# Modulation vectors on TensorE, or on VectorE from weights that the DMA has turned

## The chip, the core and the metric

The kernel runs on one core of a Trainium2 chip. Its time is the device time of one execution in microseconds (us); lower is better. TensorE multiplies matrices and writes PSUM, VectorE and ScalarE read PSUM back and do elementwise work, GpSimd (POOL in the profile) does small elementwise work and issues some DMAs, and SyncE (SP) issues most DMAs. Each engine runs its own queue in order.

## The reference

A transformer block of 2048 tokens and width 1024: linear attention with 32 heads, then a SwiGLU feed-forward of width 3584. Both halves are modulated by six vectors of 1024 that come from one conditioning vector `c`:

```python
mod = (silu(c) @ w_mod).reshape(1, 6, 1, 1024)
sa, ca, ga, sb, cb, gb = ...                       # the six vectors, in this order
h = layernorm(x) * (1 + ca) + sa
x = x + ga * A(h, wqkv, wo)                        # phi(q), phi(k), kv = sum k v, o = num/den, @ wo
h = layernorm(x) * (1 + cb) + sb
x = x + gb * B(h, w_gate, w_up, w_down)            # (silu(h@w_gate) * (h@w_up)) @ w_down
```

Here `w_mod` is 1024 x 6144. The change is about how `ga`, `sb` and `cb` are computed; `sa` and `ca` are needed at the very start and keep their way, and so does `gb`.

## The kernel before

The 2048 tokens are four blocks (`sc`) of 512. Activations stand transposed (`hT`: features on partitions, tokens along the row), so a modulation vector is wanted as columns (128 partitions x 8), one scalar to a partition, and `modulate` applies it with eight VectorE instructions to a block. The exception is the gate `ga`: it is folded into the weight `wo` (`wo * ga_bc`), for which it must stand as one row that all partitions hold (`ga_bc`).

**Phases of attention.** For each block: `k_phase` (eight groups of eight matmuls; each group's PSUM accumulator is taken by ScalarE's exp and two VectorE instructions, `phi_to`), `kv_phase` of the block before (128 small matmuls into one PSUM tile, added to `kv_acc` on VectorE), `v_phase` (eight groups, taken by ScalarE alone). While a block's k and v phases run, `ln1` prepares the next block: statistics on VectorE (`bn_stats`, `veps`), `rstd` and `nmr` on POOL, the normalised tile on ScalarE, a DMA transpose into `hT`, and `modulate`. After the last block come `q_phase(1, ...)`, the last `kv_phase`, the copies `KVB` and `Zden` on VectorE from `kv_acc`, a TensorE transpose `tpk` (tile `tp`) of `KVB`, the denominators `den`, and `fold_wo`, which multiplies `wo` by the kv matrix. Only then can attention's output `wo_tile` and the feed-forward (`gate_up`, `down`) run.

**The vectors before.** `mod_load` brings blocks of `w_mod` (tile `wml`) by plain DMAs. `ga_rows` and `mod_rows` multiply them on TensorE by silu(c) spread over 32 columns (`sc32`), 32 matmuls each into PSUM tile `modr`, with ScalarE copying the result out; POOL DMAs write rows to DRAM (`mrow_dram`) and read them back, broadcast for `ga_bc` and as columns for `sbT`, `cb1T`. They stand between two groups of `k_phase`: `ga_rows` in block 2, `mod_rows` in block 3.

**What sets the order.** A list scheduler orders each engine's instructions by priority, mostly program order. `mm` keeps TensorE in program order. `tc.issue_after(x)` puts an instruction behind `x`. `in_order` fixes the first block's order on VectorE, ScalarE and POOL. Two pools of PSUM accumulators, `pa` and `pb`, have four banks each: a matmul group cannot start until the group four before it has been taken out. The large SBUF tiles share 19 buffers (`k8`); a load waits until the tile that held its buffer has had its last use.

**The start.** `keep_warm` issues matmuls of zeros (`sel`) while the first DMAs are under way, so that TensorE's clock is up when the k matmuls of block 0 begin; `mod_rows_a` computes `sa` and `ca` as their weights (`wme`) land.

Of the kernel before, what the change touches and what calls it, by code (L numbers as in the profile page):

```python
# [9 lines left out]
ALU = mybir.AluOpType  # L10
BF16 = mybir.dt.bfloat16
# [10 lines left out]
def kernel(  # L22
# [91 lines left out]
    c_sb = const.tile([DC, P], BF16, name="c_sb")  # L114

    x_tiles = {}

    def load_x(st, eng):
        x_sb = k2.tile([P, D], BF16, name="x_sb")
        eng.dma_start(out=x_sb[:], in_=x2[st * P:(st + 1) * P, :])  # L120
        x_tiles[st] = x_sb

    for st in range(STC - 1):
# [61 lines left out]
    scr = scr_t[:, 0:A * 64].rearrange("p (i q r) -> p i q r", q=2, r=32)  # L185
    sa0T, ca0T = scr[:, :, 0, 0], scr[:, :, 1, 0]
    sbT = const.tile([P, DC], F32, name="sbT")
    cb1T = const.tile([P, DC], F32, name="cb1T")
    ga_t = ep.tile([P, NB], F32, name="e")
    ga_bc = ga_t[:].bitcast(BF16)  # L190
    gb_bc = const.tile([P, D], BF16, name="gb_bc")
# [9 lines left out]
    def build_masks():  # L201
        nc.gpsimd.memset(zmask[:], 0.0)
        for h in range(HPC):
            rs = slice(h * DH, (h + 1) * DH)
            for hg in range(HG):
                nc.gpsimd.memset(zmask[rs, hg, HG * h + hg:HG * h + hg + 1], 1.0)

    def rstd_of(mv, n):
        veps = small.tile([P, STC], F32, name="veps")
        nc.vector.tensor_scalar_add(out=veps[:, 0:n], in0=mv[:, 0:n, 1], scalar1=LN_EPS)  # L210
        rstd = small.tile([P, STC], F32, name="rstd")
        nc.gpsimd.tensor_tensor(out=rstd[:, 0:n], in0=veps[:, 0:n], in1=neg_half[:].to_broadcast([P, n]), op=ALU.pow)  # L212
        return rstd
# [9 lines left out]

    def normalise_act(dst, src, mv, rstd):
        nmr = small.tile([P, 1], F32, name="nmr")
        nc.gpsimd.tensor_scalar(out=nmr[:], in0=mv[:, 0, 0:1], scalar1=rstd[:, 0:1], scalar2=-1.0,  # L226
                                op0=ALU.mult, op1=ALU.mult)
        nc.scalar.activation(out=dst, in_=src, func=ACT.Identity, bias=nmr[:], scale=rstd[:, 0:1])  # L228

# [19 lines left out]
    def ln1_norm(sc, t, x_sb, mv, rstd, dve=False):  # L249
        xn = k2.tile([P, D], BF16, name="xn", bufs=4)  # L250
        if dve:
            normalise(xn[:], x_sb[:], mv[:, 0, 0:1], rstd[:, 0:1])
        else:
            normalise_act(xn[:], x_sb[:], mv, rstd)
        if sc > 0:
            nc.sync.dma_start_transpose(hTs[sc][:, :, t * P:(t + 1) * P], xn[:])
        return xn

    def ln1(sc):
# [48 lines left out]
    def k_phase(sc, lo, hi):  # L308
        if lo == 0:
            pks[sc] = big("pk", [STC, D])  # L310
        for g in k_groups[lo:hi]:
            accs = [acc_a()]
            k_mms(sc, [g], accs)
            k_evac(sc, [g], accs)

    def v_phase(sc):
        v = big("v", [VT + DH])
# [8 lines left out]
                                     start=(cc == 0), stop=(cc == DC - 1))  # L326
                nc.scalar.copy(out=v[:, t * D + nb * NB:t * D + (nb + 1) * NB], in_=acc[:])  # L327

    def q_phase(sc, lo=0, hi=DC):
        if lo == 0:  # L330
            pqs[sc] = big("pq", [HG, SCW])
        for qc in range(lo, hi):
            acc = acc_a()
            for cc in range(DC):
                mm(acc[:], lhsT=wq[cc // 4][:, cc % 4, qc * P:(qc + 1) * P], rhs=hTs[sc][:, cc, :],
                                 start=(cc == 0), stop=(cc == DC - 1))
            phi_to(pqs[sc][:, qc, :], acc[:])

    def v_ones(v, lo):
        head = v[:, lo:lo + DH]  # L340
# [2 lines left out]
    def kv_phase(sc):  # L343
        kvp = acc_b("kvp", (HG, 2, DH))
        for hg in range(HG):
            for t in range(STC):
                for i in range(HPC):
                    mm(kvp[i * DH:(i + 1) * DH, hg, :, :], lhsT=pks[sc][:, t, hg * P + i * DH:hg * P + (i + 1) * DH],
                       rhs=v_ones(vs[sc], t * D + hg * P + i * DH), start=(t == 0), stop=(t == STC - 1))
        kvv = kvp[:].rearrange("p g k e -> p g (k e)")[:, :, 0:DH + 1]  # L350
        if sc == 0:
            nc.vector.tensor_copy(out=kv_acc, in_=kvv)
        else:
            nc.vector.tensor_tensor(out=kv_acc, in0=kv_acc, in1=kvv, op=ALU.add)

    def gb_load():
        for j in range(DC):
# [9 lines left out]
            else:  # L367
                nc.vector.scalar_tensor_tensor(out=gb_acc[:], in0=t[:], scalar=sc, in1=gb_acc[:], op0=ALU.mult, op1=ALU.add)

    def ga_rows(blks):  # L370
        ps = acc_b("modr")
        H2 = NB // 2
        for j in range(DC):
            for g in range(4):
                mm(ps[32 * g:32 * g + 32, 0:H2], lhsT=sc32[:, j, :], rhs=blks[g // 2][:, j, (g % 2) * H2:(g % 2 + 1) * H2],
                   start=(j == 0), stop=(j == DC - 1))
        row = small.tile([P, NB], BF16, name="mrow", bufs=1)
        nc.scalar.copy(out=row[:, 0:H2], in_=ps[:, 0:H2])
        for g in range(4):
            nc.gpsimd.dma_start(out=mrow_dram[0, g:g + 1, 0:H2], in_=row[32 * g:32 * g + 1, 0:H2])  # L380
        nc.gpsimd.dma_start(out=ga_bc.rearrange("p (g n) -> p g n", g=4),
                            in_=mrow_dram[0, :, 0:H2].unsqueeze(0).to_broadcast([P, 4, H2]))

    gb_rows = []

    def mod_load(cols):
        blks = []
        for lo in cols:
            t = big("wml", [DC, NB])
            nc.sync.dma_start(out=t[:], in_=wm_v[:, :, lo:lo + NB])  # L390
            blks.append(t)
        return blks

    def mod_rows(blks):
        ps = acc_b("modr")
        for j in range(DC):
            for g in range(4):
                mm(ps[32 * g:32 * g + 32, :], lhsT=sc32[:, j, :], rhs=blks[g][:, j, :],
                                 start=(j == 0), stop=(j == DC - 1))
        row = small.tile([P, NB], BF16, name="mrow", bufs=1)  # L400
        nc.scalar.copy(out=row[:], in_=ps[:])
        return row

    mrow_dram = dram.tile([2, 4, NB], BF16, name="mrow_scratch")

    def mod_spread(k, row):
        for g in range(4):
            nc.gpsimd.dma_start(out=mrow_dram[k, g:g + 1, :], in_=row[32 * g:32 * g + 1, :])
        cols = small.tile([P, 2 * DC], BF16, name="mcol", bufs=1)
        with nc.allow_non_contiguous_dma(reason="2048 elements, once"):  # L410
            nc.gpsimd.dma_start(out=cols[:], in_=mrow_dram[1].rearrange("g (i p) -> p (g i)", p=P))
        nc.vector.tensor_copy(out=sbT[:], in_=cols[:, 0:DC])
        nc.vector.tensor_scalar_add(out=cb1T[:], in0=cols[:, DC:2 * DC], scalar1=1.0)

    def modulate_all(hT, scaleT, biasT):
        for cc in range(DC):
# [40 lines left out]
    def keep_warm(acc, n):  # L457
        for _ in range(n):
            mm(acc[:], lhsT=sel[:, 0, :], rhs=sel[:], start=True, stop=True)

    gs = k_groups[0:6]
    accs = [acc_a() if i < 4 else acc_b("acc") for i in range(6)]
    spare = accs[5]
    keep_warm(spare, 9)
    hT = hTs[0] = big("hT", [DC, SCW])
    pks[0] = big("pk", [STC, D])
    H = 3 * P
    with in_order(nc.vector, nc.scalar, nc.gpsimd):
# [6 lines left out]
        st0 = ln1_stats(0, 0)  # L475
        nc.vector.tensor_copy(out=sc32[:], in_=scT[:].unsqueeze(2).to_broadcast([P, DC, 32]))
        xns = [ln1_norm(*st0)] + [ln1_norm(*ln1_stats(0, t)) for t in range(1, 3)]
        keep_warm(spare, 6)
        mod_rows_a(0)
        pe_transpose_tile(hT, xns[0], 0)  # L480
        keep_warm(spare, 3)
        mod_rows_a(1)
        pe_transpose_tile(hT, xns[1], 1)
        keep_warm(spare, 2)
# [28 lines left out]
        k_evac(0, gs8, accs8)  # L513
    with tc.issue_after(last_on[nc.gpsimd.engine]):
        build_masks()
        nc.gpsimd.tensor_copy(out=scf[:], in_=scT[:])

    for sc in range(NSC):
        if sc > 0:
            k_phase(sc, 0, 2)  # L520
            kv_phase(sc - 1)
            k_phase(sc, 2, 4)
            if sc == 2:
                ga_rows(blks)
            if sc == 3:
                mod_spread(1, mod_rows(blks))
            k_phase(sc, 4, 8)
            if sc == 1:
                blks = mod_load([2 * D, 2 * D + NB])
            if sc == 2:  # L530
                blks = mod_load([3 * D, 3 * D + NB, 4 * D, 4 * D + NB])
        v_phase(sc)
        if sc + 1 < NSC:
            with tc.issue_after(last_on[nc.vector.engine] if sc == 0 else last_phi[-5].ins):
                ln1(sc + 1)
        if sc == 0:
            q_phase(0, 0, 6)
        if sc + 1 < NSC:
            with tc.issue_after(last_phi[0].ins):
                modulate_all(hTs[sc + 1], ca1T, saT)  # L540
        if sc == 0:
            q_phase(0, 6, 8)
        if sc + 2 < NSC:
            for st in range((sc + 2) * STC, (sc + 3) * STC):
                load_x(st, nc.sync)
        if sc == 2:
            wo = [big("wo", [4, D]) for _ in range(2)]
            for h in range(2):
                for g in range(4):
                    nc.sync.dma_start(out=wo[h][g * DH:(g + 1) * DH, :, :], in_=wo_v[h, g])  # L550
            for cc in range(DC):
                w = wo[cc // 4][:, cc % 4, :]
                nc.vector.tensor_tensor(out=w, in0=w, in1=ga_bc, op=ALU.mult)

    q_phase(1, 0, 2)
    kv_phase(NSC - 1)
    nc.vector.tensor_copy(out=KVB, in_=kv_acc[:, :, 0:DH])
    nc.vector.tensor_tensor(out=Zden[:], in0=kv_acc[:, :, DH:DH + 1].to_broadcast([P, HG, DH]),
# [121 lines left out]
    for st in range(STC):  # L680
        wo_tile(st)
    q_phase(2, 6, 8)
    q_phase(3, 0, 5)
    with tc.issue_after(last_phi[0].ins):
        modulate_all(h2Ts[0], cb1T, sbT)
# [63 lines left out]
```

## Time and profile before

| | us |
|---|---|
| median of 6 runs | 836.56 (836.3 to 837.0) |
| the profiled execution, its own time | 836.86 |
| its span, first to last instruction | 835.1 |
| TensorE busy | 823.9 |
| VectorE busy | 317.2 |
| ScalarE busy | 168.6 |
| GpSimd busy | 67.5 |
| bytes moved by DMA | 129.07 MB |

The page gives each engine's busy time, a chain of work that ended last (at each step, what released it), groups of equal instructions with the mean time of one and the idle time before them, and DMA issues with the time from issue to landing. A busy engine off the chain costs nothing; time on the chain that is taken away is gained only until the next wait shows. The granted TensorE clock was 1.0 over the span.

### The profile page before, as it was taken

The numbers are of one execution on the slowest core, as the hardware profiler recorded it, in microseconds if no ns is written. First come the engines' busy times: TensorE is split into PE (matmuls) and PEld (weight loads), VectorE is DVE, ScalarE is ACT, GpSimd is POOL, SyncE is SP. The second block draws the span as 40 slices with busy tenths as digits, with TensorE's granted clock in tenths as the row PEclk, the third lists the DMA queues.
The fourth block names the chain that finished last, engine by engine and source line by source line (L and its number), as shares of the span: only waits on it lengthen the run. The fifth ranks groups of instructions, "written<-read, shape, count | busy, mean of one in ns | idle before, by whom it ended". The sixth has DMA issues, their size and how long they took to land.

```text
span 835.1 us, 11191 instructions
## 1 busy us (share of the span) xinstructions
PE 823.9 (99%) x4560; PEld 378.3 (45%) x4641; DVE 317.2 (38%) x606; ACT 168.6 (20%) x253; POOL 67.5 (8%) x168
## 2 busy tenths in 40 slices
PE   8999999999999999999999999999999999999998
PEld 3444444444444444444444444444444444444444
DVE  5755643587444325521222244211114431111122
ACT  3455343334211111101111110111110101111000
POOL 2101201111130301100000010000001100000000
PEclk9999999999999999999999999999999999999999
DMA  9873790129998544636434183672504529710011
GB/s 319 298 202 85 226 197 1 31 62 287 358 261 257 189 151 139 189 112 221 147 108 144 44 227 95 216 224 79 174 1 154 162 69 329 241 54 1 19 58 51
DMA packets 125748, 129.07 MB, mean 155 GB/s; under 512 B 34112, under 2 KB 106304, under 8 KB 125184
## 3 DMA queue, kind: packets, MB, share of 16 engines
q1 hardware_dynamic: 121440, 114.97, 45.7%
q0 software_dynamic: 3968, 12.99, 5.3%
q8 instruction: 36, 0.59, 0.3%
q10 hardware_dynamic: 288, 0.40, 0.1%
q14 instruction: 16, 0.13, 0.0%
HBM read 108.27 MB, written 12.72 MB: 145 GB/s over the span
## 4 chain that ended last, share of the span: by engine, by line
PE 97%; DMA 2%; issue 1%; DVE 0%; ACT 0%; ACTq 0%; SPq 0%
PE acc L98 89%; PE a_ps L98 7%; DMA wme<-in_w_mod_dram 2%; PE kvp L98 1%; PE modr L98 0%; PE den L98 0%; PE mod_ps L98 0%; DVE wo L577 0%; PE wf L98 0%; DVE pq L292 0%; ACT eb L289 0%; ACTq L125 0%; PE tp L101 0%; SPq L134 0%; DVE eb L290 0%
## 5 line engine op out<-in xcount | busy, mean ns | idle before, releaser
L98 PE MATMUL acc<-h2T,wgu 128*128 128x512 bf16 x1756 | 385.7, 379 | 1.9
L98 PEld LDWEIGHTS <-wgu 128*128 128x128 bf16 x1792 | 175.1, 98 | 211.5
L98 PE MATMUL acc<-wd,gu 128*128 128x512 bf16 (+2 forms) x908 | 195.2, 373 | 0.9
L646 DVE TENSOR_TENSOR gu<-acc,e 128x512 bf16<-128x512 f32 x112 | 77.4, 691 | 289.9 <-PE acc L98 278.9
L645 ACT ACTIVATE e<-acc 128x512 f32<-128x512 f32 x112 | 66.9, 597 | 374.8 <-PE acc L98 363.4
L98 PEld LDWEIGHTS <-gu 128*128 128x128 bf16 x924 | 89.3, 98 | 104.5
L98 PEld LDWEIGHTS <-hT 128*128 128x128 bf16 x512 | 49.4, 98 | 59.7 <-issue 1.0
L667 DVE TENSOR_TENSOR e<-acc,gb_bc 128x512 f32<-128x512 f32 (+2 forms) x33 | 22.3, 675 | 131.5 <-PE acc L98 122.6
L98 PE MATMUL a_ps<-wo,pq 128*128 128x512 bf16 x250 | 56.9, 379 | 0.3
L98 PE MATMUL acc<-wk,hT 128*128 128x512 bf16 x248 | 56.4, 379 | 0.6 <-issue 0.3
L98 PE MATMUL acc<-hT,wq 128*128 128x512 bf16 x247 | 55.6, 379 | 0.9 <-issue 0.6
L98 PE MATMUL acc<-wv,hT 128*128 128x512 bf16 x251 | 55.6, 379 | 0.3
L289 ACT ACTIVATE eb<-acc 128x512 bf16<-128x512 f32 x64 | 37.8, 596 | 74.7 <-PE acc L98 71.5
L228 ACT ACTIVATE xn<-x,nmr,rstd 128x1024 bf16<-128x1024 f32 x16 | 19.9, 1241 | 126.2 <-POOL nmr L226 126.2
L614 POOL DMA_DIRECT2D x_scratch<-x x16 | 9.9, 616 | 377.5 <-DVE x L607 377.5
L98 PEld LDWEIGHTS <-pq 128*128 128x128 bf16 x256 | 25.0, 98 | 30.2
L98 PEld LDWEIGHTS <-wq 128*128 128x128 bf16 x256 | 24.5, 98 | 29.9 <-issue 0.9
L290 DVE TENSOR_SCALAR eb<-eb 128x512 bf16<-128x512 bf16 x64 | 18.4, 292 | 49.0 <-ACT eb L289 49.0
L607 DVE TENSOR_TENSOR x<-a_ps,x_sb 128x512 f32<-128x512 f32 x32 | 22.1, 691 | 7.8 <-PE a_ps L98 7.0
L212 POOL TENSOR_TENSOR rstd<-veps,neg_half 128x1 f32<-128x1 f32 x32 | 17.9, 560 | 81.1 <-DVE veps L210 71.4
L327 ACT CAST v<-acc 128x512 bf16<-128x512 f32 x32 | 18.2, 582 | 22.7 <-PE acc L98 22.1
L670 DVE TENSOR_TENSOR ob<-e,x1r 128x512 bf16<-128x512 f32 (+2 forms) x33 | 22.2, 674 | 1.0
(82 smaller groups left out, 275.0 us busy)
## 6 DMA issues: line engine op xcount, KB each, us to landing
wgu<-in_B_w_gate_dram SPq DMA_DIRECT2D x28, 1024.0 KB, 7.5
wgu<-in_B_w_up_dram SPq DMA_DIRECT2D x28, 1024.0 KB, 9.1
x_sb<-in_A_x_dram SPq DMA_DIRECT2D x32, 256.0 KB, 7.2
x_scratch<-x POOLq DMA_DIRECT2D x16, 512.0 KB, 3.0
x1r<-x_scratch SPq DMA_DIRECT2D x31, 256.0 KB, 2.9
wd<-in_B_w_down_dram SPq DMA_DIRECT2D x7, 1024.0 KB, 7.1
wml<-in_w_mod_dram SPq DMA_DIRECT2D x6, 1024.0 KB, 8.9
rbc<-rden_scratch POOLq DMA_DIRECT2D x16, 256.0 KB, 8.4
```

The lines of the kernel that those rows point to most:

```text
L98: return tc.keep_in_program_order(nc.tensor.matmul(out, lhsT=lhsT, rhs=rhs, start=start, stop=stop))
L212: nc.gpsimd.tensor_tensor(out=rstd[:, 0:n], in0=veps[:, 0:n], in1=neg_half[:].to_broadcast([P, n]), op=ALU.pow)
L228: nc.scalar.activation(out=dst, in_=src, func=ACT.Identity, bias=nmr[:], scale=rstd[:, 0:1])
L289: nc.scalar.activation(out=e[:], in_=acc, func=ACT.Exp)
L290: nc.vector.tensor_scalar(out=e[:], in0=e[:], scalar1=1.0, scalar2=PHI_EPS, op0=ALU.min, op1=ALU.add)
L327: nc.scalar.copy(out=v[:, t * D + nb * NB:t * D + (nb + 1) * NB], in_=acc[:])
L607: nc.vector.tensor_tensor(out=x1[:, ns], in0=a_ps[:], in1=x_t[:, ns], op=ALU.add)
L614: nc.gpsimd.dma_start(out=x1_dram[st * P:(st + 1) * P, :], in_=x1[:])
L645: nc.scalar.activation(out=sg[:], in_=ps[0][:], func=ACT.Silu)
L646: gm = nc.vector.tensor_tensor(out=guT[sc][f // GPT][:, f % GPT, :], in0=ps[1][:], in1=sg[:], op=ALU.mult)
L667: nc.vector.tensor_tensor(out=yt, in0=y_ps, in1=gb_bc[:, ns], op=ALU.mult)
L670: nc.vector.tensor_tensor(out=ob, in0=yt, in1=x1r, op=ALU.add)
```

## The change

`ga`, `sb` and `cb` leave TensorE. `mod_load` now fetches 512 columns of `w_mod` at a time with a transposing DMA, so that each row of the tile (`wmt`) holds one output column's 1024 weights; silu(c) stands as a row that all partitions hold (`sc_row`, made at the start by eight small matmuls into `accs` and two ScalarE copies); and one VectorE instruction (`mod_step`) multiplies 128 such rows by it and sums along the row, which gives 128 elements of a vector as one column. Eight steps make a vector, 24 make the three. They are placed by hand: `V_STEPS` counts those in each block's v phase (in blocks 1 and 2 held behind the last `nmr` on POOL by a scalar `one` that POOL sets there), `K_STEPS` those behind single k groups, and two stand in `q_phase(1, ...)`. One pair of `wmt` tiles is loaded for each of the first three blocks, behind that block's `hT` transposes on SP.

`sb` and `cb` are then where they are wanted. `ga` must become a row: `ga_spread` turns its columns with a VectorE 32x32 transpose, writes 32 runs of 32 elements to DRAM in four POOL DMAs and reads them back broadcast. The load of `wo` and its multiplication by `ga_bc` move from block 2 to block 3. The warming matmuls at the start are partly replaced by f32 ones, and the kv addition is held behind the last `phi_to`.

```diff
@@ -185,7 +186,10 @@
     scr = scr_t[:, 0:A * 64].rearrange("p (i q r) -> p i q r", q=2, r=32)
     sa0T, ca0T = scr[:, :, 0, 0], scr[:, :, 1, 0]
     sbT = const.tile([P, DC], F32, name="sbT")
+    cbT = const.tile([P, DC], F32, name="cbT")
     cb1T = const.tile([P, DC], F32, name="cb1T")
+    gaT = const.tile([P, DH], F32, name="gaT")
+    sc_row = const.tile([P, D], BF16, name="sc_row")
     ga_t = ep.tile([P, NB], F32, name="e")
     ga_bc = ga_t[:].bitcast(BF16)
     gb_bc = const.tile([P, D], BF16, name="gb_bc")
@@ -253,7 +259,7 @@
-            nc.sync.dma_start_transpose(hTs[sc][:, :, t * P:(t + 1) * P], xn[:])
+            last_load[0] = nc.sync.dma_start_transpose(hTs[sc][:, :, t * P:(t + 1) * P], xn[:])
@@ -312,6 +318,7 @@
             k_evac(sc, [g], accs)
+            mod_step(int(k_groups.index(g) in K_STEPS[sc]))
@@ -326,7 +333,7 @@
-    def q_phase(sc, lo=0, hi=DC):
+    def q_phase(sc, lo=0, hi=DC, steps=0):
@@ -335,6 +342,7 @@
+            mod_step(steps)
 @@ -351,7 +359,8 @@
-            nc.vector.tensor_tensor(out=kv_acc, in0=kv_acc, in1=kvv, op=ALU.add)
+            with tc.issue_after(last_phi[0].ins):
+                nc.vector.tensor_tensor(out=kv_acc, in0=kv_acc, in1=kvv, op=ALU.add)
 @@ -367,50 +376,47 @@
             else:
                 nc.vector.scalar_tensor_tensor(out=gb_acc[:], in0=t[:], scalar=sc, in1=gb_acc[:], op0=ALU.mult, op1=ALU.add)
 
-    def ga_rows(blks):
...
+    ga_dram = dram.tile([1, D], BF16, name="ga_scratch")
+    mod_steps = []
+
+    def mod_load(q, cols):
+        for h in range(2):
+            t = big("wmt", [DC // 2, D])
+            lo = q * D + h * NB
+            last = nc.sync.dma_start_transpose(t[:], w_mod[:, lo:lo + NB])
+            mod_steps.extend((t[:, i, :], cols[:, 4 * h + i:4 * h + i + 1]) for i in range(DC // 2))
+        return last
+
+    def mod_step(n, anchor=None):
+        if n == 0:
+            return
+        scale = 1.0
+        if anchor:
+            one = small.tile([P, 1], F32, name="one", bufs=1)
+            with tc.issue_after(last_nmr[0].ins):
+                nc.gpsimd.memset(one[:], 1.0)
+            scale = one[:]
+        with tc.issue_after(anchor or last_phi[0].ins):
+            for _ in range(n):
+                rows, col = mod_steps.pop(0)
+                last = nc.vector.scalar_tensor_tensor(out=rows, in0=rows, scalar=scale, in1=sc_row[:], op0=ALU.mult,
+                                               op1=ALU.mult, accum_out=col)
+        return last
+
+    K_STEPS = [(), (), (0, 2), (0, 2, 4, 5, 6)]
+    V_STEPS = [0, 4, 4, 7]
+
+    def ga_spread():
+        turned = small.tile([P, P], F32, name="dsum", bufs=1)
+        nc.vector.transpose(out=turned[:, 0:DH], in_=gaT[:])
+        row = small.tile([P, P], BF16, name="rb", bufs=4)
+        nc.vector.tensor_copy(out=row[:, 0:DH], in_=turned[:, 0:DH])
+        cells = ga_dram[0].rearrange("(i g r) -> g i r", g=4, r=DH)
         for g in range(4):
-    def mod_load(cols):
...
-    def mod_rows(blks):
...
-    mrow_dram = dram.tile([2, 4, NB], BF16, name="mrow_scratch")
-    def mod_spread(k, row):
...
+            nc.gpsimd.dma_start(out=cells[g], in_=row[g * DH:g * DH + DC, 0:DH])
+        nc.gpsimd.dma_start(out=ga_bc, in_=ga_dram[:].to_broadcast([P, D]))
 
     def modulate_all(hT, scaleT, biasT):
         for cc in range(DC):
@@ -458,10 +464,16 @@
         for _ in range(n):
             mm(acc[:], lhsT=sel[:, 0, :], rhs=sel[:], start=True, stop=True)
 
+    def keep_warm_f32(acc, n):
+        zeros = sel[:].rearrange("p h n -> p (h n)").bitcast(F32)
+        for _ in range(n):
+            mm(acc[:, 0:zeros.shape[1]], lhsT=zeros[:, 0:P], rhs=zeros, start=True, stop=True)
+
     gs = k_groups[0:6]
     accs = [acc_a() if i < 4 else acc_b("acc") for i in range(6)]
     spare = accs[5]
-    keep_warm(spare, 9)
+    keep_warm_f32(spare, 3)
+    keep_warm(spare, 2)
     hT = hTs[0] = big("hT", [DC, SCW])
     pks[0] = big("pk", [STC, D])
     H = 3 * P
@@ -475,10 +487,14 @@
         st0 = ln1_stats(0, 0)
         nc.vector.tensor_copy(out=sc32[:], in_=scT[:].unsqueeze(2).to_broadcast([P, DC, 32]))
         xns = [ln1_norm(*st0)] + [ln1_norm(*ln1_stats(0, t)) for t in range(1, 3)]
-        keep_warm(spare, 6)
+        keep_warm_f32(spare, 3)
         mod_rows_a(0)
         pe_transpose_tile(hT, xns[0], 0)
-        keep_warm(spare, 3)
+        for h in range(2):
+            for j in range(DC // 2):
+                mm(accs[h][:, j * P:(j + 1) * P], lhsT=scT[:, 4 * h + j:4 * h + j + 1].to_broadcast([P, P]), rhs=ident[:],
+                   start=True, stop=True)
+            nc.scalar.copy(out=sc_row[:, h * NB:(h + 1) * NB], in_=accs[h][:])
         mod_rows_a(1)
         pe_transpose_tile(hT, xns[1], 1)
         keep_warm(spare, 2)
@@ -513,28 +529,35 @@
         k_evac(0, gs8, accs8)
     with tc.issue_after(last_on[nc.gpsimd.engine]):
         build_masks()
+        nc.gpsimd.memset(gaT[:], 0.0)
         nc.gpsimd.tensor_copy(out=scf[:], in_=scT[:])
 
     for sc in range(NSC):
         if sc > 0:
             k_phase(sc, 0, 2)
             kv_phase(sc - 1)
-            k_phase(sc, 2, 4)
-            if sc == 2:
-                ga_rows(blks)
-            if sc == 3:
-                mod_spread(1, mod_rows(blks))
-            k_phase(sc, 4, 8)
-            if sc == 1:
-                blks = mod_load([2 * D, 2 * D + NB])
-            if sc == 2:
-                blks = mod_load([3 * D, 3 * D + NB, 4 * D, 4 * D + NB])
+            if sc == NSC - 1:
+                wo = [big("wo", [4, D]) for _ in range(2)]
+                for h in range(2):
+                    for g in range(4):
+                        with tc.issue_after(last_load[0].ins):
+                            nc.sync.dma_start(out=wo[h][g * DH:(g + 1) * DH, :, :], in_=wo_v[h, g])
+            k_phase(sc, 2, 8)
         v_phase(sc)
         if sc + 1 < NSC:
             with tc.issue_after(last_on[nc.vector.engine] if sc == 0 else last_phi[-5].ins):
                 ln1(sc + 1)
         if sc == 0:
             q_phase(0, 0, 6)
+        steps = mod_step(V_STEPS[sc], last_veps[0].ins if sc + 1 < NSC else None)
+        if sc == NSC - 1:
+            with tc.issue_after(steps.ins):
+                for cc in range(DC):
+                    w = wo[cc // 4][:, cc % 4, :]
+                    nc.vector.tensor_tensor(out=w, in0=w, in1=ga_bc, op=ALU.mult)
+        if sc == 2:
+            with tc.issue_after(last_veps[0].ins):
+                ga_spread()
         if sc + 1 < NSC:
             with tc.issue_after(last_phi[0].ins):
                 modulate_all(hTs[sc + 1], ca1T, saT)
@@ -543,16 +566,12 @@
         if sc + 2 < NSC:
             for st in range((sc + 2) * STC, (sc + 3) * STC):
                 load_x(st, nc.sync)
-        if sc == 2:
-            wo = [big("wo", [4, D]) for _ in range(2)]
-            for h in range(2):
-                for g in range(4):
-                    nc.sync.dma_start(out=wo[h][g * DH:(g + 1) * DH, :, :], in_=wo_v[h, g])
-            for cc in range(DC):
-                w = wo[cc // 4][:, cc % 4, :]
-                nc.vector.tensor_tensor(out=w, in0=w, in1=ga_bc, op=ALU.mult)
-
-    q_phase(1, 0, 2)
+        if sc + 1 < NSC:
+            with tc.issue_after(last_load[0].ins):
+                last_load[0] = mod_load(*((2, gaT), (3, sbT), (4, cbT))[sc])
+
+    q_phase(1, 0, 1, 2)
+    q_phase(1, 1, 2)
     kv_phase(NSC - 1)
     nc.vector.tensor_copy(out=KVB, in_=kv_acc[:, :, 0:DH])
     nc.vector.tensor_tensor(out=Zden[:], in0=kv_acc[:, :, DH:DH + 1].to_broadcast([P, HG, DH]),
@@ -680,6 +699,7 @@
     for st in range(STC):
         wo_tile(st)
     q_phase(2, 6, 8)
+    nc.vector.tensor_scalar_add(out=cb1T[:], in0=cbT[:], scalar1=1.0)
     q_phase(3, 0, 5)
     with tc.issue_after(last_phi[0].ins):
         modulate_all(h2Ts[0], cb1T, sbT)
```

More of the change, by code (lines that the diff above doesn't have):

```diff
@@ L116 @@
     x_tiles = {}
+    last_load = [None]
     def load_x(st, eng):
         x_sb = k2.tile([P, D], BF16, name="x_sb")
-        eng.dma_start(out=x_sb[:], in_=x2[st * P:(st + 1) * P, :])
+        last_load[0] = eng.dma_start(out=x_sb[:], in_=x2[st * P:(st + 1) * P, :])
         x_tiles[st] = x_sb
@@ L206, in build_masks @@
                 nc.gpsimd.memset(zmask[rs, hg, HG * h + hg:HG * h + hg + 1], 1.0)
+    last_veps, last_nmr = [None], [None]
     def rstd_of(mv, n):
         veps = small.tile([P, STC], F32, name="veps")
-        nc.vector.tensor_scalar_add(out=veps[:, 0:n], in0=mv[:, 0:n, 1], scalar1=LN_EPS)
+        last_veps[0] = nc.vector.tensor_scalar_add(out=veps[:, 0:n], in0=mv[:, 0:n, 1], scalar1=LN_EPS)
         rstd = small.tile([P, STC], F32, name="rstd")
@@ L225, in normalise_act @@
         nmr = small.tile([P, 1], F32, name="nmr")
-        nc.gpsimd.tensor_scalar(out=nmr[:], in0=mv[:, 0, 0:1], scalar1=rstd[:, 0:1], scalar2=-1.0,
+        last_nmr[0] = nc.gpsimd.tensor_scalar(out=nmr[:], in0=mv[:, 0, 0:1], scalar1=rstd[:, 0:1], scalar2=-1.0,
                                 op0=ALU.mult, op1=ALU.mult)
@@ L368, in gb_sum @@
                 nc.vector.scalar_tensor_tensor(out=gb_acc[:], in0=t[:], scalar=sc, in1=gb_acc[:], op0=ALU.mult, op1=ALU.add)
-    def ga_rows(blks):
-        ps = acc_b("modr")
-        H2 = NB // 2
-        for j in range(DC):
-            for g in range(4):
[L375 to L378, printed above, removed]
-        for g in range(4):
-            nc.gpsimd.dma_start(out=mrow_dram[0, g:g + 1, 0:H2], in_=row[32 * g:32 * g + 1, 0:H2])
-        nc.gpsimd.dma_start(out=ga_bc.rearrange("p (g n) -> p g n", g=4),
-                            in_=mrow_dram[0, :, 0:H2].unsqueeze(0).to_broadcast([P, 4, H2]))
@@ L384 @@
-    gb_rows = []
-    def mod_load(cols):
[L387 to L392, printed above, removed]
-    def mod_rows(blks):
[L395 to L402, printed above, removed]
@@ L404 @@
-    mrow_dram = dram.tile([2, 4, NB], BF16, name="mrow_scratch")
-    def mod_spread(k, row):
[L407 to L413, printed above, removed]
+    gb_rows = []
@@ L545 @@
                 load_x(st, nc.sync)
-        if sc == 2:
-            wo = [big("wo", [4, D]) for _ in range(2)]
-            for h in range(2):
-                for g in range(4):
-                    nc.sync.dma_start(out=wo[h][g * DH:(g + 1) * DH, :, :], in_=wo_v[h, g])
-            for cc in range(DC):
-                w = wo[cc // 4][:, cc % 4, :]
-                nc.vector.tensor_tensor(out=w, in0=w, in1=ga_bc, op=ALU.mult)
-    q_phase(1, 0, 2)
+        if sc + 1 < NSC:
[3 more added lines that the diff above has]
+    q_phase(1, 1, 2)
     kv_phase(NSC - 1)
```

## The prediction

> **What bounds the kernel now.** I read the page's engine totals first, then the chain that ended last in order of time, then busy time by stage, then the groups by shape, and last the DMA issues.
>
> ```profile
> span 835.1 us, 11191 instructions
> PE 823.9 (99%) x4560; PEld 378.3 (45%) x4641; DVE 317.2 (38%) x606; ACT 168.6 (20%) x253; POOL 67.5 (8%) x168
> ...
> 7.64 6.94 DMA wme<-in_w_mod_dram
> 14.62 0.51 PE mod_ps L98 x8
> ...
> 95.89 0.99 PE modr L98 x32
> ...
> 125.87 1.84 PE modr L98 x32
> ...
> 153.30 3.40 PE acc L98 x15
> 156.70 0.11 PE tp L101 x2
> 156.81 0.56 PE den L98 x32
> ```
>
> TensorE is the bound: 99% busy, and the chain is matmuls almost without a gap. So taking matmuls out pays one to one, and any VectorE work costs nothing until TensorE waits for it. Two places in the chain matter. The first 14.6 us end with a DMA (the first modulation weights), not with TensorE. And the two `modr` pieces, 0.99 and 1.84 us, lie bare on the chain; they are what the change takes off. Behind the second of them `tp` (156.70) and `den` (156.81) follow the q matmuls at once: today nothing waits there.
>
> ```profile
> 118.00:135.00 17.00, 16.73 (x223) 7.95 (x225) 11.79 (x23) 5.33 (x10) 3.32 (x6) 1.00 0.33 74
> 135.00:149.00 14.00, 13.95 (x65) 6.33 (x65) 1.13 (x4) 4.88 (x9) 0.00 (x0) 1.00 0.01 1
> 149.00:161.00 12.00, 11.63 (x221) 6.03 (x222) 7.32 (x16) 3.17 (x7) 1.14 (x3) 1.00 0.01 3
> ...
> L292 DVE SCALAR_TENSOR_TENSOR pq<-acc,eb 128x512 bf16<-128x512 f32 x32 | 21.8, 689 | 1.0
> L368 DVE SCALAR_TENSOR_TENSOR x<-x_sb,scf,x 128x1024 f32<-128x1024 bf16 x4 | 5.1, 1282 | 0.1
> L453 DVE TENSOR_TENSOR pq<-pq,rbc 128x1024 bf16<-128x1024 bf16 x16 | 9.9, 682 | 0.0
> L553 DVE TENSOR_TENSOR wo<-wo,e 128x1024 bf16<-128x1024 bf16 x8 | 5.0, 684 | 2.9 <-DMA wo<-in_A_wo_dram 2.9
> L412 DVE CAST sbT<-mcol 128x8 f32<-128x8 bf16 x1 | 0.2, 171 | 2.0 <-DMA mcol<-mrow_scratch 2.0
> ...
> hT<-xn SPq DMA_TRANSPOSE x12, 3.5
> ```
>
> The third number pair after the stage's length is VectorE: 1.13 us of work in the 14 us of the last v phase. That is the hole the change fills. The rows below price its new instructions.
>
> **The change part by part.** *Removed.* 64 matmuls on `modr`, with their weight loads, two ScalarE copies, ten POOL DMAs and two small VectorE copies. The matmuls are worth 0.99 + 1.84 = 2.83 us of chain; five POOL DMAs of the new ga route replace the ten. A later stall at 168.8 (`fold_wo` waits for ScalarE and VectorE) follows TensorE's own q matmul, so it moves along and takes none of this back.
>
> *Added on VectorE.* 24 steps `wmt*sc_row` with a column sum: 4 in the v phase of block 1, 2+4 in block 2, 5+7 in block 3, 2 in `q_phase(1)`. Call s the start-to-start time of one. The trace has no such form. Below: if it went at the rate of `L453` (spaced 0.60 back to back), 0.60. Above: the 1282 ns of `L368` plus the 171 ns of a narrow op (`L412`), 1.45. Between them, the scalar of the last 14 is a constant, as in `L292`: 689 ns for 512 elements is 533 at 0.96 per ns and about 150 fixed, so 1024 elements take 1.22 us, and successors start 0.08 early, as they do in `L453`: 1.14. Here a rule speaks against the change. The Trainium skill, "VectorE: DVE Perf Modes", section "Two Vector instructions with no wait between them", says that an op which also writes out its accumulator is two instructions. No run shown here has one; by a narrow op (0.08 start to start, 0.17 alone) it makes s 1.22 to 1.31. I take 1.26.
>
> *Blocks 1 and 2.* 4s = 5.0 us fit block 1's idle stretch before `modulate` (6.4 us, ended by hT's DMA), even with about 1.0 us in which the first step waits for POOL's `rstd`, `nmr` and the new `one`. In block 2 the two steps among the k groups push the last `veps` from 105.8 to about 107.6, and with it the last normalised tile and hT's turn; by the present 3.8 us from tile to `modulate`, this starts near 114.2, the four steps end then too, and the k phase that needs it starts at 116.6: 2 us of cover. Behind it the eight `modulate` are consumed no faster than produced. PSUM banks: the third v group needs the bank of the seventh k group at 106.2, freed about 105.5. Cost 0; if this cover is gone (s near 1.5) some tenths.
>
> *Block 3, where it can stall.* TensorE runs 0.99 us earlier than today up to the fourth k group and 2.83 after. VectorE spends 0.94 per evacuation (`L290` and `L292`, start to start) and is saturated from the fifth k group, whose evacuation ends at 128.3. Then come three evacuations (2.8), three steps, seven steps, eight `wo` multiplies (8 x 0.61 = 4.9), one evacuation, two steps, one evacuation with `cb1T` (1.0), the kv sum (0.45), `KVB` (0.2): `KVB` ends at 128.3 + 10.3 + 12s + about 0.1 for the first wait. TensorE reaches `tp`, which needs it, at 156.54 - 2.83 = 153.7, and `den`, which needs `Zden` 0.4 after `KVB`, at 153.9. So the stall is 0.84 at s = 1.30, 12 us per us of s around it, zero below 1.23: 0.36 at 1.26. By the row alone (1.14) it would be 0, by the rule's upper end 0.96. Queued behind it on VectorE are two evacuations and the first reciprocal; they have a stretch of 3.4 us of q matmuls in which to catch up.
>
> *DMA and queues.* SP issues two transposes of 1 MB for two plain loads (0.6 us each, or 6.0 for four); hT's take 1.23 us of SP for a quarter of that, so about 4.9 each, in stretches where SP waits for ScalarE anyway (49.6 to 73.9; 83 to 102.6; after 110). `wo`'s eight loads move behind the last pair, from 104 to about 121, land by some 133 and are needed at 144; their two buffers are freed by ga's steps and by block 2's kv sums, both before. On POOL ga's five DMAs run from about 114.5 (present ones: 0.5 us to issue, 1.5 and 4.7 to land) and are done near 124. Cost 0. The transposes' landing is a rival below.
>
> *Start.* 15 bf16 warming matmuls become six f32 ones and two bf16 ones; three more make way for eight small ones and two ScalarE copies, done near 13.1, before `accs` is written at 15.9. The `sel` matmuls are 0.43 apart up to 6.5 us and 0.21 after. An f32 one is not in the trace: between one pass (256 columns, 0.21 slow) and four, as "FP8 and Floating Point Precision" (TensorE Precision Notes) says, 0.85. By four passes the first batch is 3.4 us against today's 3.8; by one pass 1.5, and TensorE might stay slow for longer. What covers it: the weights land at 14.6 either way, so no gain; the loss lies between 0 and 1.5. I take 0.1, nearest to the present spacing.
>
> **Sum.** -2.83 + 0.36 + 0.1 = -2.4 us. The profiled execution took 836.86 us (span 835.1), 0.3 above the median of the six runs; against the median, 836.56 - 2.4 = 834.2.
>
> **The rivals.** *No stall:* s below 1.23, or the bf16 rate. 836.56 - 2.83 + 0.1 = 833.8. For it: the hole of 13 us. Against it: `L368`, and the second instruction.
>
> *The gain eaten at KVB:* s = 1.45 gives 2.6 us of stall: 836.5. For it: every form with a column sum is unknown. Against it: the fixed part of narrow ops is small.
>
> *Slower: cb's turned weights late.* Its two transposes are issued near 111 and the fifth cb step needs the second at about 141, so 15 us each are covered, and above 17 each the kernel is slower by more than 0.2%, one to one, since the steps block VectorE's evacuations. hT's 256 KB land in 3.5 us; four times that is 14, and h2T's worst, 7.7 under load, would make 31. Against it: 3.5 us holds a fixed part, and 1.23 us of issue per 256 KB suggests some 7. At 20 us each: about 844.
>
> *The clock at the start late by 3 us:* 1.5 us lost, 835.6.
>
> **How the numbers follow.** 0.2% is 1.67 us, about what a measurement of this kernel can tell from no change. Forecast (s 1.23 to 1.33) 0.46; no stall 0.20; gain mostly eaten 0.17; late weights or an overloaded VectorE beyond s = 1.6 (4.4 us of stall) 0.14; late clock 0.03. Faster: forecast and no stall, 0.66; same: the eaten and late-clock cases, 0.20; slower 0.14. The range goes from 833.4 (no stall and nothing lost at the start, 833.7, less 0.3 of scatter) to 837.4, past the eaten case. Most of the slower case lies outside.
>
> **What would show it.** No `modr` rows; the step's mean under 1.35 us; a TensorE wait of under 1 us before `tp` or `den` near 154; no wait before the k phases at 87 and 117; `wmt` landing in under 12 us; first k matmul at 15.9. Wrong if `tp` waits over 2 us for `KVB`, if a step waits for a `wmt` DMA, or if `sel`'s slow spacing reaches past 8 us.

## The result, and the profile after

| | before | after |
|---|---|---|
| median, us (all runs) | 836.32 (36 runs) | 833.96 (16 runs, 833.4 to 834.6) |
| the profiled execution, its own time | 836.86 | 833.99 |
| its span | 835.1 | 832.1 |

The ratio is 0.9971, with a 95% interval of 0.9965 to 0.9978: the change takes 2.4 us off (1.8 to 2.9). The sum had said -2.4. But it was made of other terms than those that the chip added up, and this is what the experiments are about.

First the page of the kernel after (engine totals), then its chain of waits in order of time (start, length, what), over the last two blocks of attention and up to the first denominators:

```profile
span 832.1 us, 11105 instructions
PE 820.7 (99%) x4502; PEld 378.9 (46%) x4581; DVE 344.7 (41%) x655; ACT 168.7 (20%) x253; POOL 64.4 (8%) x166
...
90.38 1.15 PE kvp L98 x128
91.53 0.16 issue
91.69 10.74 PE acc L98 x49
...
119.26 1.30 PE kvp L98 x128
120.56 0.16 issue
120.72 1.24 PE acc L98 x5
121.96 0.57 issue
122.53 9.67 PE acc L98 x44
...
150.35 3.40 PE acc L98 x15
153.75 0.11 PE tp L101 x2
153.86 0.56 PE den L98 x32
```

The `modr` pieces are gone, and `tp` and `den` follow the q matmuls at once, as they did before. `den` starts at 153.86 instead of 156.81, and from there to the end both executions take 678.3 us; so the whole difference arises ahead of it. One line is new: 0.57 us of "issue" at 121.96, in which TensorE waits for nothing that the profile shows. It stands just after the burst `kvp` of 128 small matmuls, which itself takes 1.30 us where the other bursts take 1.15. The same place in the kernel before:

```profile
121.16 1.15 PE kvp L98 x128
122.31 0.16 issue
122.47 3.40 PE acc L98 x15
```

Next the stage of the last v phase (length, then busy time and count for TensorE, its weight loads, VectorE, ScalarE and POOL, then clock, DMA share and GB/s), and the VectorE groups by shape:

```profile
135.00:149.00 14.00, 13.95 (x69) 6.18 (x71) 13.31 (x25) 4.69 (x8) 0.00 (x0) 1.00 0.01 1
...
L404 DVE SCALAR_TENSOR_TENSOR wmt<-wmt,sc_row 128x1024 bf16<-128x1024 bf16 x16 | 18.9, 1216 | 0.0
L404 DVE SCALAR_TENSOR_TENSOR wmt<-wmt,one,sc_row 128x1024 bf16<-128x1024 bf16 x8 | 9.8, 1280 | 2.3 <-POOL one L399 2.3
L404 DVE DVE_READ_ACCUMULATOR wmt<-wmt,sc_row 128x1 f32 x16 | 1.3, 81 | 0.0
```

The hole of the last v phase (135 to 149) is full: 13.31 us of VectorE where there were 1.13. A step is indeed two instructions, 1216 ns and an accumulator read of 81 ns. How they lie in time decides their price; the VectorE timeline of the kernel after, at the last two steps and the copies that TensorE needs (start, length, what):

```profile
148.91 1.22 DVE L404 SCALAR_TENSOR_TENSOR wmt<-wmt,sc_row 128x1024 bf16<-128x1024 bf16 x1
150.05 0.08 DVE L404 DVE_READ_ACCUMULATOR wmt<-wmt,sc_row 128x1 f32 x1
150.05 1.22 DVE L404 SCALAR_TENSOR_TENSOR wmt<-wmt,sc_row 128x1024 bf16<-128x1024 bf16 x1
151.20 0.08 DVE L404 DVE_READ_ACCUMULATOR wmt<-wmt,sc_row 128x1 f32 x1
...
152.58 0.29 DVE L576 CAST kvs<-kvs 128x256 bf16<-128x256 f32 x1
152.79 0.42 DVE L577 TENSOR_TENSOR Zden<-kvs,zmask 128x256 bf16<-128x256 f32 x1
```

The read starts at 150.05, before its step has ended, and the next step starts at 150.05 too. Start to start a step takes 1.147 us, not 1.216 plus 0.081. `KVB` (L576) is done at 152.87 and `Zden` at 153.21, ahead of `tp` at 153.75 and `den` at 153.86.

### The profile page after: what moved, and what is told of

It reads as the page before. It is cut to its first block, busy times and chain, and to the rows that moved or that the text cites. A ratio compares the mean times of both kernels' runs of the same rounds, so it can differ in the third digit from the quotient of the medians.

```text
span 832.1 us, 11105 instructions
## 1 busy us (share of the span) xinstructions
PE 820.7 (99%) x4502; PEld 378.9 (46%) x4581; DVE 344.7 (41%) x655; ACT 168.7 (20%) x253; POOL 64.4 (8%) x166
## 4 chain that ended last, share of the span: by engine, by line
PE 98%; DVE 1%; issue 1%; ACT 0%; POOL 0%
PE acc L98 90%; PE a_ps L98 7%; PE kvp L98 1%; DVE stats L224 0%; PE mod_ps L98 0%; PE den L98 0%; ACT xn L234 0%; DVE wo L596 0%; PE tp L101 0%; PE wf L98 0%; DVE pq L298 0%; ACT eb L295 0%; POOL rstd L218 0%; DVE mv L225 0%; DVE veps L216 0%
## 5 line engine op out<-in xcount | busy, mean ns | idle before, releaser
L627 DVE BATCH_NORM_STATS2 stats<-x 128x6 f32<-128x512 f32 x32 | 22.2, 694 | 1.1
```

The lines of the kernel that those rows point to most:

```text
L627: nc.vector.bn_stats(out=stats[:, nb, :], in_=x1[:, ns])
```

## The experiments

Theory: the time is the bare `modr` matmuls, less whatever TensorE waits for elsewhere. Rivals: the gain came from the start, where the first k matmul went from 15.94 to 15.16; or VectorE's slack at `KVB` is much more, or less, than the timeline shows; or the new order costs something that the chain doesn't name.

**The warming matmuls.** One run puts the bf16 ones back into the kernel after, the other puts the f32 ones alone into the kernel before.

```diff
-    keep_warm_f32(spare, 3)
-    keep_warm(spare, 2)
+    keep_warm(spare, 9)
...
-        keep_warm_f32(spare, 3)
+        keep_warm(spare, 6)
```

> The changed kernel with the bf16 warming matmuls of before (9 and 6) in place of the six f32 and two bf16 ones; all else as changed. The profile after had its first k matmul at 15.16 us, before at 15.94. Theory A, the f32 warmers bring the start forward: 0.8 us slower than the changed kernel, about 834.7, and the first k matmul back near 15.9. Theory B, the 0.8 us is scatter in when the first weights land: the same as the changed kernel within 0.3 us, 834.0.

> The kernel before with the f32 warming matmuls alone (3 f32 + 2 bf16, then 3 f32). Theory A, they bring the start forward: 0.8 us faster than before, 835.5. Theory B, scatter in the landing of the first weights: the same as before within 0.3 us, 836.3.

Measured: 833.86 (ratio to before 0.9973, 0.9962 to 0.9983) and 836.17 (0.9997, 0.9988 to 1.0006). Neither differs from the kernel that it was made from. In the profiles the first k matmul stands at 15.43 and 15.16. So f32 against bf16 moves the start by 0.27 us in the profile and by nothing that the medians show; the rest of the 0.78 between the two first profiles is scatter (a kernel before with fewer matmuls, below, starts its k groups at 15.44). The start is not the gain.

**The slack at `KVB`, from both sides.** Three more steps behind the last seven, on rows already used, into unused columns of `gaT`; and all twelve steps of block 3 in the v phase, none among the k groups.

```diff
+            for i in range(extra):
+                last = nc.vector.scalar_tensor_tensor(out=rows, in0=rows, scalar=scale, in1=sc_row[:], op0=ALU.mult,
+                                               op1=ALU.mult, accum_out=gaT[:, DC + i:DC + i + 1])
```

```diff
-    K_STEPS = [(), (), (0, 2), (0, 2, 4, 5, 6)]
-    V_STEPS = [0, 4, 4, 7]
+    K_STEPS = [(), (), (0, 2), ()]
+    V_STEPS = [0, 4, 4, 12]
```

> The changed kernel with three further VectorE steps behind the seven of the last v phase (they repeat the last step into a column that nothing reads; cb's tile is spoilt for nothing else). In the profile after, KVB ends 0.9 us before tp needs it and Zden 0.65 us before den does. Theory, VectorE's queue up to KVB has 0.65 us of cover left: 3 x 1.147 - 0.65 = 2.8 us of TensorE wait before den, 836.8. Rival, the queue has more slack than that (evacuations slip into it): under 1 us, 834.9 or less.

> The changed kernel with the five steps behind block 3's k groups moved into its v phase (twelve there); no work added. Theory, the placing decides, because the v phase's hole is 13 us and 12 x 1.147 + 4.9 (wo) = 18.7 us do not fit: counted on from the last k evacuation at about 133.5, Zden ends near 157.6 where den could start at 153.9, so 3.7 us of wait, 837.7, slower than before. Rival, VectorE's total work is what counts and it is the same: 834.0.

Measured: 837.53 (1.0010, 1.0001 to 1.0019) and 838.17 (1.0020, 1.0011 to 1.0029). What TensorE waits for from 60 to 178 us (in total, times, longest), in the kernel after and then in the one with three more steps:

```profile
PE acc L98 <- issue: 1.5, 7, 0.6
PE wf L98 <- DVE wo L596: 0.2, 1, 0.2
```

```profile
PE tp L101 <- DVE kvs L579: 2.0, 1, 2.0
PE acc L98 <- issue: 0.5, 1, 0.5
PE wf L98 <- DVE wo L599: 0.2, 1, 0.2
```

With three more steps `KVB` ends 2.88 us later (155.75) and `tp` waits 1.99; with all steps in the v phase it waits 2.96. So the theory holds in kind: what stands on VectorE ahead of `KVB` decides, since the second kernel has the same VectorE work in all. In size it was too strict (2.8 and 3.7 were expected). In the kernel after VectorE still has a hole ahead of `KVB`, in which it waits for ScalarE, and the added work fills that first:

```profile
147.98 0.29 DVE L296 TENSOR_SCALAR eb<-eb 128x512 bf16<-128x512 bf16 x1 [0.66 <-ACT eb L295]
```

The hole of 0.66 and the 0.65 us by which `Zden` is ahead of `den` make about 1.3 us of slack: one more step of 1.147 would just fit and two would not (an estimate; neither was run). The three added steps, all on the same rows, stand 1.27 us apart, not 1.147.

The two medians are 1.6 and 1.3 us above after plus wait. The profile of the kernel with three more steps shows why: behind the wait TensorE's granted clock is halved for 3.4 us, which costs 1.7 (two stretches of it; the clock is the third number from the right):

```profile
156.00:158.00 2.00, 1.96 (x37) 1.11 (x36) 1.93 (x6) 0.00 (x0) 0.00 (x0) 0.50 0.00 0
158.00:160.00 2.00, 2.00 (x8) 0.79 (x7) 1.29 (x3) 0.00 (x0) 0.38 (x1) 0.65 0.00 0
```

Six of this kernel's ten runs have a mean clock of 0.998 and take 837.3 to 838.2; the three at 1.0 take 835.8 to 836.7. With all steps in the v phase the profiled execution keeps its clock behind the wait and takes 837.0, while the five runs at 0.997 or 0.998 take 838.6 to 839.2.

**The matmuls alone.** The kernel before with 8 of its 64 `modr` matmuls.

```diff
-        for j in range(DC):
+        for j in range(1):
```

> The kernel before with one eighth of the matmuls on modr (j = 0 alone, 8 of 64), so that ga, sb and cb are partial sums; loads, copies, POOL DMAs and everything else stay. Theory: the modr matmuls lie bare on TensorE's chain and are worth their 0.99 + 1.84 us one to one: 7/8 of 2.83 is 2.5 us, 833.8. Rival: something else (the wait at fold_wo, the row's way through DRAM) gives part of it back: under 1.5 us faster.

Measured: 835.93 (0.9994, 0.9985 to 1.0003), 0.5 us less than the 836.4 of before, where the theory wanted 2.5 (the rival's number, though not for a reason that it named).

**The transposes alone:** plain loads of the same size in the kernel after.

```diff
-            last = nc.sync.dma_start_transpose(t[:], w_mod[:, lo:lo + NB])
+            last = nc.sync.dma_start(out=t[:], in_=wm_v[:, 4 * h:4 * h + 4, q * D:(q + 1) * D])
```

> The changed kernel with the six transposing loads of w_mod replaced by plain loads of as many bytes into the same tiles (so ga, sb and cb are sums over the wrong weights). Theory, the turned loads are covered: the same time within 0.3 us, 834.0; SP's issue falls from 9 us to some 1.5 us a pair. Rival, the transposes' small packets hold up something, such as TensorE's 0.57 us of issue at 122 that only the profile after shows: 0.6 us faster, 833.4, and that gap gone.

Measured: 835.55 (0.9997, 0.9988 to 1.0005), slower than after by 1.6 us; neither theory nor rival had that. (Seven of the eleven runs take 834.4 to 835.7; four, with a mean clock of 0.997 or 0.998, take 837.5 to 837.9.) Both misses show the same line in the chain of waits. First the kernel with fewer `modr`, then the one with plain loads:

```profile
119.87 1.15 PE kvp L98 x128
121.02 1.40 PE acc L98 x6
122.42 1.58 issue
124.00 2.32 PE acc L98 x10
```

```profile
119.26 1.15 PE kvp L98 x128
120.41 1.40 PE acc L98 x6
121.81 2.28 issue
124.09 26.51 PE acc L98 x122
```

Six matmuls after the burst TensorE stands still for 1.58 and 2.28 us, its operands ready and its accumulators free. It is the "issue" line of the kernel after, grown. And it accounts for both: 2.28 us of `modr` pieces taken away (2.83 less the 0.55 left) less 1.58 is 0.7; and 2.28 less after's 0.72 (0.57, and 0.15 in the burst) is 1.56 us, where 1.6 was measured.

**What TensorE waits for.** The profile's DMA queues hold one that is not the kernel's: q8, kind "instruction", 36 packets of 16 KB on the page of after. TensorE has some 9,100 matmuls and weight loads, so a packet is about 256 of them. The Trainium skill, "Runtime: NRT & Kernel Launch", section "Instruction fetch mechanics", says that an engine's program is brought in blocks of 16 KiB, 256 instructions, by a DMA queue of its own. That fits the rows. It also calls the cost mostly hidden, because an engine issues more slowly than the blocks arrive. At `kvp` that does not hold: 128 matmuls and 128 loads, a whole block, go by in 1.15 us, while the packet alone takes 1.07 (of the large matmuls, 0.22 us each, a block lasts 28 us). The start of the packet in question by the trace's DMA records, and when the matmuls go on:

| kernel | burst starts | packet starts | takes | matmuls again | gap |
|---|---|---|---|---|---|
| after | 119.26 | 120.02 | 1.07 | 122.53 | 0.57 |
| after, bf16 warming | 119.53 | 120.43 | 1.13 | 122.95 | 0.97 |
| before, 8 `modr` | 119.87 | 121.48 | 1.12 | 124.00 | 1.58 |
| after, plain loads | 119.26 | 121.23 | 1.35 | 124.09 | 2.28 |
| before | 121.16 | 113.28 | 0.92 | no gap | 0 |

In each kernel with a gap the matmuls go on 1.4 to 1.5 us after the packet is in. In the kernel before, the packet comes 8 us ahead of the burst. If the place in the program decides when it is asked for, then more instructions at the start must move it. `pad` does this in four kernels: 32 matmuls of zeros (with their loads, 62 instructions net), worth about 0.1 us.

```diff
+    def pad(acc, n):
+        for i in range(n):
+            g = 32 * (i % 4)
+            mm(acc[g:g + 32, 0:64], lhsT=sel[:, 0, 0:32], rhs=sel[:, 1, 0:64], start=True, stop=True)
...
-        keep_warm(spare, 5)
+        pad(spare, 32)
+        keep_warm(spare, 4)
```

> The changed kernel with 32 tiny matmuls (zeros, 128x32 weights, 64 columns) in place of one of the five warming matmuls before the fourth set of modulation rows: 62 more TensorE instructions ahead of the k groups, about 0.1 us of work. Theory (program fetch): TensorE's program comes in pieces of 16 KB, and the gap of 0.57 us at 121.96 (with the kv burst of block 2 at 1.30 instead of 1.15 us) is TensorE waiting for the piece that landed at 121.1, which it asks for at a fixed place in the program, just ahead of the burst; moved by 62 instructions, the piece is asked for some 6 us earlier, gap and stretch go, 834.0 becomes 833.3. Rival (the transfers around 120 alone delay TensorE, wherever it is in its program): the gap stays, 834.0.

> The changed kernel with plain loads in place of the turned ones (as in the run e5_plain_loads, so that the later modulation vectors are not the reference's) and the same 32 tiny matmuls. Theory (program fetch): the gap of 2.28 us at 121.81 goes and the time falls from 835.55 to about 833.3; plain loads then cost no more than turned ones. Rival: the gap stays, 835.5.

> The kernel before with 8 of its 64 modr matmuls (as in the run e4_before_fewer_modr, so that the later modulation vectors are not the reference's) and the same 32 tiny matmuls. Theory (program fetch): the gap of 1.58 us at 122.42 goes and the time falls from 835.93 to about 834.4, which leaves the matmuls taken away worth about 2 us, as the sum had it. Rival: the gap stays, 835.9, and the modr matmuls were never worth more than 0.5 us.

| kernel | without `pad` | with `pad` | ratio to before with `pad` |
|---|---|---|---|
| after | 833.96 | 833.43 | 0.9965 (0.9952 to 0.9977) |
| after, plain loads | 835.55 | 833.26 | 0.9964 (0.9951 to 0.9978) |
| before, 8 `modr` | 835.93 | 833.86 | 0.9968 (0.9956 to 0.9981) |

DMA queues of the kernel after from 119 to 122 us (packets, MB, share of 16 engines), and of the padded one from 112 to 121 and from 109 to 112:

```profile
q1 hardware_dynamic: 1733, 0.44, 120.5%
q8 instruction: 1, 0.02, 2.2%
```

```profile
q1 hardware_dynamic: 7979, 2.17, 109.6%
```

```profile
q1 hardware_dynamic: 1047, 0.34, 110.8%
q8 instruction: 1, 0.02, 2.2%
```

The packet now comes at 109.97, ten microseconds ahead of the burst (119.70) (in all four padded kernels it comes between 109.97 and 111.12, 74 to 84 recorded TensorE instructions ahead), with the hardware queue nearly as full (111% of the engines against 120%), and the gap is gone from the chain of the padded kernel with plain loads:

```profile
119.42 1.15 PE kvp L98 x128
120.57 0.16 issue
120.73 10.74 PE acc L98 x49
```

The rival (full queues alone, wherever TensorE is in its program) falls: plain loads with `pad` win 2.3 us and the few `modr` 2.1, with intervals that do not overlap those without. After alone wins 0.5 where 0.7 was expected. The intervals of these two overlap, so this one by itself shows little; its profile also has 0.39 us of new waiting for `modulate` ahead of the burst.

With the gap out of the way both misses resolve. Taking 56 of the 64 matmuls out of the kernel before is worth 2.55 us (836.41 to 833.86; their rows say 2.28). The kernel before was not run with `pad`; from 20 to 178 us its trace has no "issue" wait above 0.2 us that `pad` could take away. And turned or plain loads make no difference (833.43 and 833.26).

**The hold on POOL's `one`.** The kernel after without the scalar that keeps the steps of blocks 1 and 2 behind `nmr`.

```diff
-            scale = one[:]
```

> The changed kernel without the scalar that POOL sets: the steps of blocks 1 and 2 start right behind the last veps, beside POOL's rstd and nmr. Theory, two-input VectorE work keeps POOL waiting, so rstd and nmr run late: their 0.55 + 0.26 us stretch by some us, the last hT turn and modulate come as much later, and past the 2 us of cover TensorE waits: 834.0 to 836.5. Rival, POOL is not disturbed: steps start 1.1 us earlier, the same time, 834.0.

Measured: 836.61 (1.0000, 0.9991 to 1.0009): all of the gain is gone. POOL's timeline in block 1, first of the kernel after, then without the hold (the last pair `rstd`, `nmr`):

```profile
77.56 0.55 POOL L218 TENSOR_TENSOR rstd<-veps,neg_half 128x1 f32<-128x1 f32 x1 [0.58 <-DVE veps L216]
78.21 0.26 POOL L232 TENSOR_SCALAR nmr<-mv,rstd 128x1 f32<-128x1 f32 x1
```

```profile
77.58 1.39 POOL L218 TENSOR_TENSOR rstd<-veps,neg_half 128x1 f32<-128x1 f32 x1 [0.58 <-DVE veps L216]
79.07 1.83 POOL L232 TENSOR_SCALAR nmr<-mv,rstd 128x1 f32<-128x1 f32 x1
```

Beside the steps, POOL's two tiny instructions take 3.2 us instead of 0.8. ScalarE waits for them with `xn`, the copies of the v groups queue behind it, and TensorE waits 0.95 us for an accumulator at 82.70; in block 2 the matmuls ahead of the burst take 4.40 instead of 3.62, and the gap after it is 0.91. The Trainium skill, "SBUF — State Buffer", section "Who interferes with whom", has VectorE and GpSimd share a port pair under an exclusive lock; a VectorE instruction with two inputs in SBUF, as a step is, contends with a GpSimd instruction that reads SBUF. The two rows agree; that it is the port, no run here shows.

**A version that beats both.** The stall at `fold_wo` (about 0.7 us in both kernels: TensorE waits for ScalarE and VectorE behind the last q group of a part) goes if the fourth q group of block 2 stands ahead of the last fold.

```diff
-    q_phase(2, 2, 3)
+    q_phase(2, 2, 4)
     fold_wo(1, 1)
...
-    q_phase(2, 3, 4)
```

> The changed kernel with the fourth q group of block 2 put before the last fold_wo on TensorE instead of behind it. In both profiles this fold waits some 0.7 us for VectorE to clear PSUM banks. Theory: the group's 1.7 us of matmuls cover the wait: 0.7 us faster than the changed kernel, 833.3. Rival: VectorE's copies move behind the added evacuation and the wait stays or returns at wo_tile: the same, 834.0.

> The changed kernel with the third part of the q phase of block 2 ahead of the last fold of wo (as in the run e8_q_before_fold) and the same 32 tiny matmuls. Theory (program fetch): the two gains add, 833.43 less 0.7 is 832.7. Rival: no change against e8_q_before_fold, 833.4.

Measured: 833.43 (0.9963, 0.9950 to 0.9975) and with `pad` 832.72 (0.9956, 0.9943 to 0.9968; runs of 832.3 to 833.1, all below the lowest of after, 833.4). The first alone is not clear of after (833.96; the intervals overlap). The second is the fastest of the study, 1.2 us under after.

## Why the prediction was right, and where it was not

- *The `modr` matmuls, -2.83:* right. Alone, without the fetch gap, 56 of the 64 gave 2.55 us, where 7/8 of 2.83 is 2.5.
- *The stall at `KVB`, +0.36:* the mis-sized term; it is 0. I took s = 1.26, by adding a narrow instruction for the accumulator to the row's 1.14; it is 1.147, since the read overlaps its step's end and the next one's start. The rule on the second instruction was true (81 ns, 24 times) and the row alone had the time: spacing comes from start to start, not from a sum of durations. With `one` as scalar it is 1.206.
- *The start, +0.1:* nothing measurable.
- *What I left out:* where TensorE's program blocks fall. With the 64 `modr` matmuls and their loads out of its stream, a block's arrival moved from 8 us ahead of a burst to 0.8 us after its start, for 0.72 us in the profile. So -2.83 + 0.72 = -2.1 stands where I wrote -2.83 + 0.36 + 0.1 = -2.4, against a measured -2.4 (1.8 to 2.9). (In the two profiles `den` comes 2.95 us earlier; less the 0.78 of the start, which is scatter, 2.2.) That the total was right was partly luck: a stall that did not come stood in for one that I had not seen.
- *The rivals.* No stall at `KVB` was the true one of the four for that place. The turned weights landed in 6.4 to 8.1 us, not 15, and were never waited for. The clock at the start was not late: the warming matmuls stand 0.21 to 0.22 us apart from 6.3 us on, in the kernel before from 6.8.
- *Blocks 1 and 2, cost 0:* right in time (`modulate` at 83.93 and 113.88; I said 114.2), but I named the hold on POOL only as a wait of about 1 us. Without it the change is worth nothing.

The signs named in advance: no `modr` rows; steps under 1.35 us; no wait before `tp` or `den` at all; `wmt` in under 12 us; first k matmul at 15.16 instead of 15.9. Of the waits, "no wait before the k phases" held and the gap just after was not on the list.

## What to carry to other kernels

Price a step that VectorE repeats by the start-to-start spacing of the nearest row, and count how many steps are left before the engine behind it waits: here about one. A wait of TensorE can cost more than its own length, by the clock behind it. When matmuls are taken out and the gain is missing, look for "issue" lines on TensorE next to bursts of tiny matmuls, and at the instruction queue's packets there; a few dozen dummy instructions earlier in the program tell whether a block arrives late. Before VectorE work with two SBUF inputs is moved beside small GpSimd instructions, see who waits for those.

## What was not expected of the hardware

- TensorE can run out of program: a burst of 128 matmuls with 128 loads uses a block in 1.15 us, and a block that starts to arrive 0.8 to 2.0 us after the burst began left gaps of 0.6 to 2.3 us. Why it starts later in some kernels (0.76 us with turned loads, 1.97 with plain ones, from the same burst at 119.26) stays open: when TensorE asks for it is not in the trace. That full queues delay it (DMA share above 1.0 around 120 in all of these) was only argued.
- Behind a wait of 1.99 us TensorE's clock was halved for 3.4 us in one profile. Mean clocks of 0.997 or 0.998 appear in four of eleven, six of ten and five of ten runs of the three kernels in which TensorE, once under way, waits 2.28, 1.99 and 2.96 us at once, and in no run of the other experiments, whose longest such wait is 1.58. Why in some executions and not in others stays open.
- An f32 warming matmul of 256 columns appears as two matmul records of 557 ns mean, which start 0.43 us apart; so one takes 0.85, as the prediction's estimate by four passes had it. Three of them with two bf16 ones take 3.78 us, where nine bf16 of 512 columns take 4.02.
- A transposing load of 1 MB from DRAM takes SP 4.4 us to issue (6.1 at most) and lands in 7.2, about as fast as the plain load (6.9 in the kernel with plain loads, 8.2 in that with `pad`).
